# Awaiting the output's landing behind the closing barrier of the block instead of inside it

## The chip, the cores and the metric

The kernel runs on one core of one Trainium2 chip. The metric is the device time of one execution in microseconds (us), which is a little longer than the span of the profile: the span reaches from the first to the last of the program's own instructions, and the time also has what the runtime runs around them. Before the change the median of four runs is 420.90 us (420.85 to 422.17).

Five engines work side by side, each on its own stream of instructions: TensorE (PE in the profile, with its weight loads as PEld), VectorE (DVE), ScalarE (ACT), GpSimd (POOL) and SyncE (SP). They are ordered by semaphores alone. SP computes nothing here; it issues every transfer (DMA) of the kernel.

## What is computed

One decoding step of a transformer block for two sequences: a conditioned layer norm, attention of 32 query heads over a cache of 32768 positions in 4 groups, an output projection, a second conditioned layer norm and a two-layer mixer with gelu.

```python
mod = (_silu(c) @ w_mod).reshape(2, 6, 1, -1)      # sa, ca, ga, sb, cb, gb
h = _layernorm(x) * (1 + ca) + sa
x = x + ga * _A_ref(h, k_cache, v_cache, wq, wo)   # softmax(q k^T / sqrt(128)) v, then wo
h = _layernorm(x) * (1 + cb) + sb
return x + gb * _B_ref(h, w1, b1, w2, b2)          # gelu(norm(h) w1 + b1) w2 + b2
```

The caches are 2 x 4 x 32768 x 128 in bf16 for keys and values each, which with the weights makes 178.28 MB to be read. The output is 2 x 1 x 1024 in bf16, 4 KB.

## The kernel before

The program is recorded first and emitted afterwards. A `Tracker` takes each operation with the regions that it reads and writes, works out the semaphore waits, and keeps a list for each of the five engines. At the end `T.emit(block)` (line 734) writes every list into its engine's section of one block, opened at line 733. Each engine's section ends in a branch to a common closing part. There the engines meet in a barrier: PE, DVE, ACT and SP each count up a "gather" semaphore, POOL waits until it has all four, then counts up a "release" semaphore, on which the four leave. This closing part is written by the block itself, so the profile gives its instructions line 733. A barrier of the same build stands at the program's start, under line 748.

The work falls into a head (conditioning vector, first layer norm, projection to queries), a loop over the 8 pairs of sequence and group, in which PE, DVE and ACT each run the same recorded round, and a tail (output projection, second layer norm, mixer). SP's list is straight: it issues the loads in order, each as soon as the part of the buffer that it overwrites is free.

The tail is the part that the change touches. The last weights arrive on SP's queue as four tiles of `w2`; the last 12 of the 28 rows of blocks are multiplied at line 719 into `psO`. Then comes a chain in which each step waits for the one before: line 722 multiplies by the gate (DVE), line 723 adds the residual (DVE), line 724 transposes through PE, line 726 copies the 16 x 128 result to `res16`, which lies in the place of the input `c` and so is named `c` in the profile. SP waits for that copy and issues the one transfer to the output (line 730), whose landing counts the semaphore `s_out` up to 16. The next entry of SP's list, line 731, waits for `s_out` to reach 16. It is the last in SP's section, and in the built program this wait is carried by SP's branch out of the section, so the profile shows it under line 733. What follows it on SP is the closing barrier.

```python
T.wait("sp", reads=["res16"])
T.raw("sp", lambda e: e.dma_start(out..., res16[:, :]).then_inc(s_out, 16))   # line 730
T.raw("sp", lambda e: e.wait_ge(s_out, 16))                                   # line 731
with nc.Block() as block:                                                     # line 733
    T.emit(block)                                                             # line 734
```

Of the kernel before, what the change touches and what calls it, by code (L numbers as in the profile page):

```python
# [233 lines left out]
def bass_adaLN_cond__gqa_block_cached__mixer_channel_mlp__decode_kernel(  # L234
# [15 lines left out]
    T = Tracker(nc)  # L250
# [477 lines left out]
    s_out = nc.alloc_semaphore("s_out")  # L728
    T.wait("sp", reads=["res16"])
    T.raw("sp", lambda e: e.dma_start(out.rearrange("b o (k p) -> (b o k) p", p=128), res16[:, :]).then_inc(s_out, 16))  # L730
    T.raw("sp", lambda e: e.wait_ge(s_out, 16))

    with nc.Block() as block:
        T.emit(block)


# [26 lines left out]
```

## Time and profile before

| What | us | Where it is read |
|---|---|---|
| Median of four runs | 420.90 | the times |
| The profiled execution's own time | 420.84 | the times |
| Its span | 419.04 | the views of the trace by stretch |
| Time outside the span | 1.80 | the difference |
| PE busy | 282.1 | the page, part 1 |
| DVE busy | 169.5 | the page, part 1 |
| ACT busy | 167.6 | the page, part 1 |
| POOL busy | 6.8 | the page, part 1 |
| Stretch 40 to 375 us: DMA share 1.00, 433 GB/s | 335.0 | the stretches |
| Stretch 413.00 to 417.30 us: PE 3.11 busy, DMA share 0.38 | 4.30 | the stretches |
| Stretch 417.30 to 419.04 us: no compute engine busy, DMA share 0.01 | 1.74 | the stretches |

The profile is of one execution. "Busy" counts compute instructions alone; branches, waits on semaphores and the issue of transfers are work of an engine's sequencer and stand under the engine's name with a q behind it (SPq, POOLq). The last stretch of the table therefore shows nothing in the compute columns although something takes place in it: it is seen only in the view of one source line and in the view of waits.

### The profile page before, as it was taken

The page shows a single profiled execution, that of the slowest core. Times are in us where ns is not written, and L with a number is a line of the kernel's source. Part 1 is how long each engine was busy: PE and PEld are TensorE (multiplying, and loading weights), DVE is VectorE, ACT ScalarE, POOL GpSimd, SP SyncE. Part 2 cuts the span into 40 slices and gives each one's busy share as a digit, 9 for nine tenths or more (in the row PEclk, how much of TensorE's full clock was granted, in tenths as well). Part 3 has the DMA queues.
Part 4 walks back from the last instruction along what each step waited for, and adds up shares of the span by engine and source line. Part 5 has one row for each costly group of instructions (what it writes and reads, how often), then busy time and mean ns, then how long its engine had stood idle before and what let it go on. Part 6 is the DMA issues. An engine that isn't in the chain of part 4 may idle for free.

```text
span 419.0 us, 11662 instructions
## 1 busy us (share of the span) xinstructions
PE 282.1 (67%) x5183; PEld 223.7 (53%) x5183; DVE 169.5 (40%) x351; ACT 167.6 (40%) x275; POOL 6.8 (2%) x29
## 2 busy tenths in 40 slices
PE   1407439855992898389559928974894699274456
PEld 1104219842991498169529915972793299122324
DVE  1201105641772377157417724760673177220421
ACT  2000015544566165526545662645465266600100
POOL 3000000000000000000000000000000000000000
PEclk9976568966996799599869968995997699686565
DMA  9989999999999999999999999999999999999995
GB/s 376 450 378 446 447 404 488 409 400 445 460 413 429 438 435 429 438 435 457 410 416 475 432 394 447 460 413 429 454 419 429 438 435 457 404 422 441 416 435 232
DMA packets 5583, 178.43 MB, mean 426 GB/s; under 512 B 699, under 2 KB 707, under 8 KB 965
## 3 DMA queue, kind: packets, MB, share of 16 engines
q1 hardware_dynamic: 5572, 178.28, 98.7%
q8 instruction: 8, 0.13, 0.1%
q14 instruction: 3, 0.02, 0.0%
HBM read 178.28 MB, written 0.00 MB: 425 GB/s over the span
## 4 chain that ended last, share of the span: by engine, by line
PE 56%; DMA 22%; ACT 7%; issue 7%; DVE 7%; SPq 0%; ACTq 0%
PE psKT L534 29%; PE psZ L576 11%; DMA K<-in_A_k_cache_dram 10%; DMA w<-in_B_w_dram 9%; PE psS L546 6%; PE psZ L546 5%; ACT E_sb L566 4%; DMA wmod<-in_w_mod_dram 4%; DVE msum L591 2%; ACT KT_sb L538 2%; DVE m1c L551 1%; ACT S_sb L550 1%; PE psM L584 1%; PE psM L562 1%; PE psM L596 1%
## 5 line engine op out<-in xcount | busy, mean ns | idle before, releaser
L534 PE MATMUL psKT<-ident,K 128*128 128x128 bf16 x2048 | 154.7, 221 | 4.6 <-DMA K<-in_A_k_cache_dram 4.6
L538 ACT ACTIVATE KT_sb<-psKT 128x1024 bf16<-128x1024 bf16 x96 | 97.7, 1025 | 115.2 <-PE psKT L534 115.2
L540 DVE COPY KT_sb<-psKT 128x1024 bf16<-128x1024 bf16 x160 | 106.3, 688 | 44.1 <-PE psKT L534 43.1
L534 PEld LDWEIGHTS psKT<-ident,K 128*128 128x128 bf16 x2048 | 118.9, 98 | 5.8 <-DMA K<-in_A_k_cache_dram 4.7
L546 PE MATMUL psS<-qcur,KT_sb 128*128 128x8 bf16 x1024 | 44.3, 167 | 1.6 <-issue 1.6
L576 PE MATMUL psZ<-V,E_sb 128*32 128x512 bf16 x512 | 44.9, 528 | 0.0
L546 PE MATMUL psZ<-qcur,KT_sb 128*128 128x8 bf16 x1024 | 43.0, 167 | 0.7
L566 ACT ACTIVATE E_sb<-S_sb,negm 128x256 bf16<-128x256 f32 x64 | 32.5, 508 | 25.0 <-DVE negm L563 23.2
L546 PEld LDWEIGHTS psS<-qcur,KT_sb 128*128 128x128 bf16 x1024 | 39.2, 96 | 1.6 <-issue 1.6
L546 PEld LDWEIGHTS psZ<-qcur,KT_sb 128*128 128x128 bf16 x1024 | 37.9, 97 | 1.8 <-ACT KT_sb L538 1.2
L584 PE MATMUL psM<-onesf,rsum 128*128 128x1 f32 x16 | 4.7, 361 | 45.3 <-DVE rsum L583 45.3
L576 PEld LDWEIGHTS psZ<-V,E_sb 128*32 128x32 bf16 x512 | 17.0, 128 | 24.0 <-issue 20.0
L584 PEld LDWEIGHTS psM<-onesf,rsum 128*128 128x128 f32 x16 | 4.0, 309 | 46.1 <-DVE rsum L583 46.1
L589 DVE TENSOR_SCALAR msum<-psZ,mk 128x128 f32<-128x128 f32 x8 | 2.8, 351 | 43.1 <-PE psZ L576 43.1
L583 DVE COPY rsum<-rowsum 128x128 f32<-128x128 f32 x8 | 1.8, 227 | 41.4 <-ACT E_sb L566 41.4
L467 PE MATMUL psS<-wmod,inT 128*32 128x512 bf16 x32 | 4.9, 597 | 16.1 <-DMA wmod<-in_w_mod_dram 16.1
L551 DVE TENSOR_REDUCE m1c<-psZ 128x8 f32<-128x512 f32 x16 | 11.1, 693 | 10.3 <-ACT S_sb L550 10.3
L596 PE MATMUL psM<-msum,hmat 128*128 128x128 f32 x16 | 3.9, 326 | 13.0 <-DVE msum L591 13.0
L434 ACT ACTIVATE stat<-stat 128x2 f32<-128x2 f32 x3 | 0.6, 204 | 29.7 <-DVE stat L433 29.7
L551 DVE TENSOR_REDUCE m1c<-psS 128x8 f32<-128x512 f32 x16 | 11.1, 693 | 3.2 <-ACT S_sb L550 3.1
L557 PE MATMUL psM<-identf,m 128*8 128x128 f32 x16 | 3.4, 296 | 13.1 <-DVE m L554 13.1
L550 ACT ACTIVATE S_sb<-psZ 128x512 f32<-128x512 f32 x16 | 9.5, 595 | 6.3 <-PE psZ L546 6.3
(121 smaller groups left out, 173.0 us busy)
## 6 DMA issues: line engine op xcount, KB each, us to landing
K<-in_A_k_cache_dram SPq DMA_DIRECT2D x16, 4096.0 KB, 25.1
wq<-in_A_wq_dram SPq DMA_DIRECT2D x2, 4096.0 KB, 45.0
wo<-in_A_wo_dram SPq DMA_DIRECT2D x2, 4096.0 KB, 36.4
w<-in_B_w_dram SPq DMA_DIRECT2D x2, 3584.0 KB, 30.6
wmod<-in_w_mod_dram SPq DMA_DIRECT2D x1, 6144.0 KB, 29.7
w<-in_B_w_dram SPq DMA_DIRECT2D x3, 2048.0 KB, 35.5
wmod<-in_w_mod_dram SPq DMA_DIRECT2D x1, 4608.0 KB, 15.7
wmod<-in_w_mod_dram SPq DMA_DIRECT2D x1, 1536.0 KB, 5.9
```

The lines of the kernel that those rows point to most:

```text
L467: pe(lambda e, w=it.view, k=k, kk=kk, ch=ch, n=n, q=q: e.matmul(bank[n][32 * q:32 * q + 32, :], lhsT=inT[:, k, :], rhs=w[:, kk, ch * 512:( ...
L534: pe(lambda e, kq=kq, jj=jj, w=kt, t=t: e.transpose(psKT[kq][:, jj * 128:(jj + 1) * 128], w[:, t, :], ident[:, :]), reads=[it.reg, "ident" ...
L538: act(lambda e, src=src: e.activation(KT_sb[g8][:, :, :], src, ACT.Copy), reads=[f"psKT{kq}"], writes=[f"KT_sb{g8}"], sem=f"ev{cc}_{g8}")
L540: dve(lambda e, src=src: e.tensor_copy(KT_sb[g8][:, :, :], src), reads=[f"psKT{kq}"], writes=[f"KT_sb{g8}"], sem=f"ev{cc}_{g8}")
L546: pe(lambda e, t=t, jj=jj: e.matmul(ps[:, t * HPG:(t + 1) * HPG], lhsT=KT_sb[g8][:, jj, :], rhs=qcur[:, :], start=True, stop=True), reads= ...
L550: act(lambda e: e.activation(Sc, ps.rearrange("p (t h) -> p h t", h=HPG), ACT.Copy), reads=[preg], writes=[f"S_sb_{cc}"], sem=f"sc{cc}")
L551: dve(lambda e: e.tensor_reduce(m1c[:, :, cc], ps.rearrange("p (t h) -> p h t", h=HPG), AX.X, ALU.max), reads=[preg], writes=[f"m1c{cc}"])
L566: act(lambda e: e.activation(E_sb[:, :, h, :], S_sb[:, h, :].rearrange("p (u t) -> p u t", t=4), ACT.Exp, bias=negm[:, h:h + 1], scale=SCA ...
L576: pe(lambda e, t4=t4, tg=tg, q=q: e.matmul(psO[32 * q:32 * q + 32, :], lhsT=E_sb[:, tg // 4, :, :].rearrange("p h t -> p (h t)"), rhs=vt[: ...
L584: pe(lambda e: e.matmul(psM[:, 144:145], lhsT=rsum16.rearrange("p g h e -> p (g h e)"), rhs=onesf[:, 0:1], start=True, stop=True), reads=[ ...
L591: dve(lambda e, q=q: e.scalar_tensor_tensor(out=msum[:, :], in0=psO[:, q * 128:(q + 1) * 128], scalar=mk4[:, q:q + 1], in1=msum[:, :], op0 ...
L596: pe(lambda e: e.matmul(psM[:, 256:384], lhsT=hmat.rearrange("p g h e -> p (g h e)"), rhs=msum[:, :], start=True, stop=True), reads=["hmat ...
```

## The change

Line 731 is taken out of SP's list. The wait for `s_out` is now an instruction of its own on SP, behind the block and so behind the block's closing barrier. The block is opened with `no_gpsimd_drain=True`.

```diff
     T.raw("sp", lambda e: e.dma_start(out.rearrange("b o (k p) -> (b o k) p", p=128), res16[:, :]).then_inc(s_out, 16))
-    T.raw("sp", lambda e: e.wait_ge(s_out, 16))
-
-    with nc.Block() as block:
+
+    with nc.Block(no_gpsimd_drain=True) as block:
         T.emit(block)
+    nc.sync.wait_ge(s_out, 16)
```

In the built program the two differ in the closing part alone. Before, PE, DVE, ACT and SP each have one DRAIN there, which itself waits for the release semaphore to be zero and counts up the gather semaphore, and one semaphore instruction (EVENT_SEMAPHORE) that waits for the release; POOL has a DRAIN and two semaphore instructions. After, each of the four has a bare DRAIN, then a semaphore instruction that counts up the gather, then the one that waits for the release; POOL has its two semaphore instructions and no DRAIN; and SP has, as its last, the wait for `s_out`. SP's branch carries no wait any more. All that stands ahead of the closing part is the same on every engine, in the same order.

## Prediction

> **What bounds the kernel now.** I read the page first, for the bulk:
>
> ```profile
> DMA  9989999999999999999999999999999999999995
> q1 hardware_dynamic: 5572, 178.28, 98.7%
> ```
>
> The sixteen DMA engines are busy in every slice but the last, 98.7% of the span on SP's queue. The kernel is bound by reading 178.28 MB; no line of that part is touched. Only the last slice ends on something else, so I went on to the timeline of the end (start, duration, engine, line):
>
> ```profile
> 413.31 2.84 PE L719 MATMUL psZ<-gT,w 128*128 128x2 bf16 x96 [0.39 <-DMA w<-in_B_w_dram]
> ...
> 416.18 0.17 DVE L722 TENSOR_TENSOR mT<-psZ,modT 128x16 f32<-128x16 f32 x1 [5.19 <-PE psZ L719]
> ...
> 416.99 0.28 DVE L726 CAST c<-psM 16x128 bf16<-16x128 f32 x1 [0.37 <-PE psM L724]
> 417.29 0.35 SPq L730 DMA_DIRECT2D out_dram<-c  x1
> ```
>
> From 413.31 all is one chain: last matmuls, two DVE steps, a transpose, a copy, and the output's issue at 417.29. There the timeline stops, but the span runs to 419.04. The view of SP's own waits and that of line 730 show what fills the 1.75 us:
>
> ```profile
> SPq L733 <- DMA out_dram<-c: 1.0, 1, 1.0
> SPq L733 <- PEq L733: 0.2, 1, 0.2
> ```
> ```profile
> DMA to landing us min/median/max: 1.4/1.4/1.4
> ```
>
> The transfer lands 1.4 us after the start of its issue, at 418.7; the issue itself took 0.35, so SP stood 1.0 us at its branch. The view of line 733 (count, then shortest/median/longest in ns, then starts) has the closing part:
>
> ```profile
> L733 POOLq EVENT_SEMAPHORE  x2: 17/17/17, 418.9 to 418.9; - x2
> L733 POOLq DRAIN  x1: 341/341/341, 374.8 to 374.8; - x1
> L733 ACTq DRAIN  x1: 279/279/279, 404.0 to 404.0; - x1
> L733 PEldq DRAIN  x1: 325/325/325, 416.7 to 416.7; - x1
> L733 DVEq DRAIN  x1: 316/316/316, 417.0 to 417.0; - x1
> L733 SPq COMPARE_BRANCH  x1: 33/33/33, 418.7 to 418.7; - x1
> L733 SPq DRAIN  x1: 7/7/7, 418.8 to 418.8; - x1
> L733 SPq EVENT_SEMAPHORE  x1: 17/17/17, 419.0 to 419.0; - x1
> ```
>
> The order in time is the point. POOL, ACT, PE and DVE arrive at the barrier at 375.1, 404.3, 417.0 and 417.3 and wait. SP is last: branch at 418.7, DRAIN at 418.8, POOL's two instructions at 418.9, release at 419.0. The barrier lies wholly behind the landing, in series with it.
>
> **The change, part by part.**
>
> The wait leaves SP's branch. Branch, DRAIN and barrier then follow the issue at once. The issue ends at 417.29 + 0.35 = 417.64. From the branch to the end of the barrier the rows show 419.04 - 418.67 = 0.37 us (the trace's records give the branch's start as 418.670 and the end as 419.041). So the barrier is over near 417.64 + 0.37 = 418.01, and with the added semaphore instruction on SP near 418.05; I price that one at 0.04 us, between its own 17 ns and the 78 ns between the starts of POOL's two in the same records. DVE, the last of the others, has arrived at 417.3, and its own added instruction at some 0.04 keeps it well ahead of SP. The cover over all this is the landing, due at 418.65 (the sixteenth count of the output's semaphore); 0.6 us of it are left. If that cover were gone, the added instructions would cost some 0.1 us.
>
> The wait comes back behind the barrier. SP reaches it near 418.05, and the landing ends it at 418.65; a semaphore instruction takes 17 ns and starts as the branch did, 17 ns after the last count. New end of the span: 418.67 + 0.02 = 418.69. **Inside the span: 419.04 - 418.69 = 0.35 us less.** Queued behind the waiting instruction on SP is nothing of the program, only the runtime's closing code, and for SP's arrival in that the other engines wait. The output's transfer is issued at the same time, past no other transfer.
>
> The drain left out on POOL: 341 ns at 374.8, 44 us before the end, under the DMA-bound tail. Nothing, either way. The same goes for PE, DVE and ACT, where DRAIN and count are now two instructions.
>
> Outside of the span lie 420.84 - 419.04 = 1.80 us, which no row of the views shows. Bounds: if the runtime's closing takes as long from SP's end as before, the gain stays 0.35. But four engines now leave near 418.05, 0.64 us ahead of SP, and can do their share of arriving in the runtime's own closing barrier under the landing. Here a rule is weighed. The trace's semaphore records run on past the span: the runtime's barrier counts one semaphore nine times from 419.28 to 419.82, 0.54 us, and the same nine counts after the semaphores' reset take 0.36 (420.61 to 420.96). The Trainium skill's "Runtime: NRT & Kernel Launch", section "The ~15µs preamble/postamble breakdown", prices the closing barrier at about 1.5 us, the reset at 1.5 and the last barrier at 2, 5 us in all; by it, up to 1.5 us of "wait for all engines" might be had. The records leave 0.54 for that barrier, of which 0.18 is more than the second takes (one count comes after 0.21 instead of 0.04). I take the records: a late arrival of one engine costs at most 0.18 plus the hops ahead of SP, say 0 to 0.3, **0.15 taken**, since which engine is late isn't told by them. Sum: 0.35 + 0.15 = 0.50 us.
>
> The second rule speaks against the change. The skill's "Runtime: NRT & Kernel Launch", "Instruction fetch mechanics", says that a taken branch to a target outside the fetched window has to fetch it before going on. The row: 33 ns of branch, then DRAIN 0.16 us after the branch's start. By the rule a fetch would cost something like the 1.4 us of the output's small transfer (an estimate), and SP's barrier would end near 417.64 + 1.4 + 0.25 = 419.3, past the landing and 0.25 later than now: 421.2. Before, such a fetch could have hidden in the wait that the branch carried only if the fetch needs no decision of the branch. By the row it ends at 418.05. I take the row: the branch goes to the same place, and the 0.16 us after it stood behind the wait.
>
> **Forecast.** The profiled 420.84 would become 420.34. The median stands 0.06 above it, so I say 420.4.
>
> **Rivals.**
>
> *SP's DRAIN sees the output in flight.* The drains of PE, DVE and ACT last 279 to 325 ns because they wait for their engine's last instruction (DVE's from 417.00 to 417.32, the copy ending at 417.27). SP's took 7 ns, but with every transfer landed. If SP's drain holds until its transfer is done, the barrier is in series again: drain over at 418.7, POOL and release 0.21 as before, plus 0.1 for the added instructions: 419.0, no gain. If it waits for more than the semaphore's last count, the Trainium skill's "DMA: Bandwidth & Descriptors" with its fixed cost of about 2.0 us for a transfer against the 1.4 measured gives 417.29 + 2.0 + 0.31 = 419.60: 0.56 slower, **421.5 us**, below the 0.3% line. It decides against the change from a drain of about 0.9 us on (417.8 to 418.7). Against it: the same page says that landing is told by the completion semaphore, and no row shows SP's sequencer knowing of a transfer otherwise. Its milder form gives 420.9.
>
> *The runtime's closing is hidden much further.* If the four early engines could also reset their semaphores under the landing, only SP's own reset and the last barrier would follow 418.69. In the records the resets fill 419.71 to 420.38, and SP's share can't be above that; some 0.9 us more would go, **419.5**. Against it: the nine counts ahead of the resets are a barrier, which SP's late arrival must hold.
>
> *Nothing shows in the time.* The span is shorter by 0.35 but the time ends on something with its own clock: **420.9**. For it only that the 1.80 us are not itemized.
>
> *The tail grows in a way no row has*, such as a fetch behind the moved wait plus a repeated closing: more than 1.3 us, **422.2**. One of the four runs of before was 422.17, so scatter can give this too.
>
> **How the numbers follow.** About 0.3%, 1.26 us, is what a measurement of this kernel can tell from no change. Forecast (420.2 to 420.6): 0.68. Drain holds SP: 0.12. Hidden further: 0.06. Nothing: 0.07. Growth or scatter above: 0.07. The range takes the first, the milder half of the second, the fourth, and the fetch that the rule would price: 420.0 to 421.2, leaving out about 0.19. Faster by over 0.3% is the third case where it reaches 1.26, and scatter: 0.06. Slower by over 0.3%: 0.07. The rest, 0.87, lies within.
>
> **What would show it.** After, SP's branch and DRAIN near 417.6 to 417.8, POOL's two instructions near 417.9, the release near 418.0, and one SP semaphore instruction with a wait of some 0.6 us on the output's transfer, ending the span at 418.7 if the bulk takes as long. It is wrong if SP's DRAIN is longer than 0.1 us, if the gap from the output's issue to the span's end stays at 1.75 instead of 1.4, or if time minus span grows from 1.80. The bulk's own length can differ between executions, so the stretch from 417.29 on is to be compared, not the span alone.

## The result and the profile after

The changed kernel takes **420.14 us** (median of 33 runs, 419.94 to 423.21), the kernel before in the same comparison 420.93 (53 runs). The ratio is 0.9981, with a 95% interval from 0.9975 to 0.9988: 0.8 us less (0.5 to 1.1), a fifth of a per cent. It is clear of no change, on the side that was forecast. The forecast was 420.4, 0.5 us less; 420.14 lies just below the band that it favoured (420.2 to 420.6) and inside its whole range (420.0 to 421.2).

The span of the profiled execution hardly tells of it. These are the first line and the DMA row of the page, after (the row is the same as before, slice by slice):

```profile
span 419.0 us, 11665 instructions
...
DMA  9989999999999999999999999999999999999995
```

The span was 419.0 before as well. But this execution issued its output later: here are the last two rows of the timeline (start, duration, engine, line).

```profile
417.27 0.28 DVE L726 CAST c<-psM 16x128 bf16<-16x128 f32 x1 [0.37 <-PE psM L724]
417.57 0.35 SPq L730 DMA_DIRECT2D out_dram<-c  x1
```

Before, the issue was at 417.29; now it is at 417.57. Those 0.28 us come from the bulk, which the change leaves alone, so each execution has to be measured from its own issue on. From the issue to the span's end it was 419.04 - 417.29 = 1.75 us, and it is 418.96 - 417.57 = 1.39.

SP's own waits, after (line, what it waited for, us in total, times, longest):

```profile
SPq L734 <- DMA out_dram<-c: 0.6, 1, 0.6
SPq L732 <- PEq L732: 0.2, 1, 0.2
```

The wait for the output is 0.6 us instead of 1.0, and stands on line 734, behind the barrier of line 732 and no longer ahead of it. The view of line 732, the closing part, and the row of line 734 (count, shortest/median/longest in ns, first and last start):

```profile
L732 DVEq EVENT_SEMAPHORE  x2: 21/21/21, 417.6 to 418.3; - x2
L732 SPq EVENT_SEMAPHORE  x2: 17/17/17, 418.2 to 418.3; - x2
L732 POOLq EVENT_SEMAPHORE  x2: 17/17/17, 418.2 to 418.3; - x2
...
L732 DVEq DRAIN  x1: 318/318/318, 417.3 to 417.3; - x1
L732 SPq DRAIN  x1: 124/124/124, 418.0 to 418.0; - x1
```
```profile
L734 SPq EVENT_SEMAPHORE  x1: 17/17/17, 418.9 to 418.9; - x1
```

The four counts of the barrier and its release are over at 418.3 to 418.4, while the output is still on its way; it lands at 418.93, and SP's wait at 418.94 is the last instruction of the program. POOL's drain is gone from the view, and so is the row of SP's branch, which now carries no wait. SP's drain has grown from 7 to 124 ns.

That is 0.36 us. The rest is outside of the span: the profiled execution took 420.26, so 420.26 - 418.96 = 1.30 us lie around it, against 1.80 before. Together 0.36 + 0.50 = **0.86 us** between these two executions, beside 0.8 between the medians. The 0.50 is no accident of one execution: over all runs of the kernel after, time less span is 1.31 us in the mean (1.25 to 1.35), and over the 35 runs of the kernel before in each later comparison 1.80 to 1.81 (1.75 to 1.85). So the larger part of the gain is not in any instruction of the program.

What runs there can be seen in the trace's records of semaphore updates, which go on past the span. There the runtime's closing barrier counts one semaphore, which no instruction of the program names, nine times; the step from one count to the next is called a hop below. The times are in us from the start of the output's issue:

```
                     1st   2nd   3rd   4th   5th   9th
before              1.988 2.022 2.234 2.278 2.301 2.525
after               1.050 1.084 1.294 1.338 1.505 1.669
```

Before, the program ended at 1.75 and all nine came after it. After, four of them come before the landing (1.36), and only five are left when SP is done at 1.39. From the ninth count to the last count of the runtime's last barrier it takes 1.14 us in both. My theory after this: the count is passed from engine to engine and back, SP is the fifth and turning one, and so a landing that SP alone waits for covers the arrival of all the others. The rivals are that the drain left out on POOL brings a part, and that it only matters how many engines arrive early, not which one is late.

### The profile page after: what moved, and what is told of

The parts are those of the page before. It is cut to its first block, busy times and chain, and to the rows that moved or that the text cites. A ratio compares the mean times of both kernels' runs of the same rounds, so it can differ in the third digit from the quotient of the medians.

```text
span 419.0 us, 11665 instructions
## 1 busy us (share of the span) xinstructions
PE 279.2 (67%) x5183; PEld 221.7 (53%) x5183; DVE 169.6 (40%) x351; ACT 167.9 (40%) x275; POOL 6.8 (2%) x29
## 4 chain that ended last, share of the span: by engine, by line
PE 56%; DMA 22%; ACT 8%; issue 7%; DVE 6%; SPq 0%; ACTq 0%
PE psKT L534 29%; PE psZ L576 11%; DMA K<-in_A_k_cache_dram 10%; DMA w<-in_B_w_dram 8%; PE psS L546 6%; PE psZ L546 5%; ACT E_sb L566 4%; DMA wmod<-in_w_mod_dram 4%; DVE msum L591 2%; ACT KT_sb L538 2%; DVE m1c L551 1%; ACT S_sb L550 1%; PE psM L584 1%; PE psM L562 1%; PE psM L596 1%
## 5 line engine op out<-in xcount | busy, mean ns | idle before, releaser
L566 ACT ACTIVATION_READ_ACCUMULATOR E_sb<-S_sb,negm 128x1 f32 x64 | 12.0, 187 | 0.0
```

Source lines behind the costliest of these rows:

```text
L566: act(lambda e: e.activation(E_sb[:, :, h, :], S_sb[:, h, :].rearrange("p (u t) -> p u t", t=4), ACT.Exp, bias=negm[:, h:h + 1], scale=SCA ...
```

## The experiments

For each kernel the table has, beside the median, three figures of its profiled execution: from the issue of the output to the span's end, the time outside of the span, and their sum, the profiled time less the start of the issue. The sum is free of the scatter of the bulk. Each ratio is to the runs of the kernel before in the same comparison; their medians were 420.93 for the change, 420.98 for the four rows below it and 420.89 for the last four. The intervals are wide, since a few runs of most kernels are 1 to 3 us above the rest, and two of the gains (wait moved alone, wait on POOL) are not clear of no change by them. Most differences here are told by the medians and the sums together, and by the time outside over all runs of a kernel, whose mean is within 0.03 us of the table's figure in every row.

| Kernel | Median | Ratio to before (95%) | Issue to span's end | Outside | Sum |
|---|---|---|---|---|---|
| before | 420.93 | | 1.75 | 1.80 | 3.55 |
| after | 420.14 | 0.9981 (0.9975 to 0.9988) | 1.39 | 1.30 | 2.69 |
| wait moved alone | 420.09 | 0.9983 (0.9965 to 1.0002) | 1.39 | 1.32 | 2.71 |
| POOL's drain left out alone | 421.01 | 1.0003 (0.9987 to 1.0020) | 1.82 | 1.79 | 3.61 |
| wait on ACT | 420.26 | 0.9980 (0.9971 to 0.9989) | 1.39 | 1.48 | 2.87 |
| wait on POOL | 420.58 | 0.9990 (0.9979 to 1.0002) | 1.38 | 1.86 | 3.24 |
| wait on PE | 420.39 | 0.9986 (0.9975 to 0.9996) | 1.43 | 1.58 | 3.01 |
| 8 counts ahead of the wait | 420.13 | 0.9984 (0.9971 to 0.9997) | 1.39 | 1.29 | 2.68 |
| 8 counts, kernel before | 420.92 | 0.9996 (0.9983 to 1.0009) | 2.17 | 1.37 | 3.54 |
| 40 counts ahead of the wait | 422.42 | 1.0037 (1.0024 to 1.0050) | 3.68 | 1.33 | 5.01 |

**The two parts of the diff apart.** First the wait is moved alone:

```diff
-    with nc.Block(no_gpsimd_drain=True) as block:
+    with nc.Block() as block:
         T.emit(block)
     nc.sync.wait_ge(s_out, 16)
```

> The wait is moved behind the block as in the change, but the block keeps its drain on POOL, so each engine's DRAIN carries the count again. Theory (the landing covers the barrier and the runtime's arrival, both through the moved wait): the whole gain is here, 0.8 us under before, 420.1; from the output's issue to the span's end 1.35 to 1.40 us instead of 1.75. Rival (leaving out POOL's drain, or the split of drain and count, brings a part): 0.2 us or more of the gain is missing, 420.4 or above.

The median is 420.09 and the sum 2.71: the whole gain is there. Ten of the twelve runs lie at or below 420.28, under the lowest of the 35 runs of before (420.73). Then POOL's drain is left out alone, in the kernel before:

```diff
-    with nc.Block() as block:
+    with nc.Block(no_gpsimd_drain=True) as block:
```

> The wait stays inside the block as before, only the drain on POOL is left out of the block. Theory: no gain; from the landing on the closing part is longer by the one added semaphore instruction on SP, so the time is 420.9 to 421.0, and SP's drain is 7 ns again since nothing is in flight. Rival (the drain left out brings a part): 420.7 or below.

It took 421.01, none of its runs is below the lowest of before, and the sum is 0.07 us longer, by the semaphore instruction that SP has more. The drains of SP on line 732 of the first and on line 733 of the second:

```profile
L732 SPq DRAIN  x1: 123/123/123, 417.8 to 417.8; - x1
```
```profile
L733 SPq DRAIN  x1: 7/7/7, 418.8 to 418.8; - x1
```

Both instructions follow everything else on SP; the one that starts 0.06 us after the end of the output's issue takes 123 ns, the one that runs after the landing 7. What the longer one waits for is open; it is over 0.83 us ahead of the landing. The rival of the drain falls: leaving it out brings nothing. The semaphore instruction that comes with it costs, if anything, the 0.07 us.

**Who waits.** The wait is given to another engine; the rest is as after the change.

```diff
-    nc.sync.wait_ge(s_out, 16)
+    nc.scalar.wait_ge(s_out, 16)
```

> As the change, but ACT waits for the output's landing instead of SP. Theory with places (the runtime's closing barrier passes a count from engine to engine, and SP stands at the turning point, so that all four ahead of it are done while it waits): ACT's late arrival holds all hops behind its own place, so 0.1 to 0.5 us of the 0.8 are lost, 420.2 to 420.7; the span is as short as after the change. Rival (only the number of engines that arrive early counts, four in both): 420.1, as after the change.

In the next kernels it is `nc.gpsimd.wait_ge` and `nc.tensor.wait_ge`.

> As the change, but POOL waits for the output's landing instead of SP. Theory with places: the trace of before and of after shows a gap of 0.21 us ahead of the third count of the runtime's closing barrier, in both, so one engine takes that much longer to arrive after the program's end; if it is POOL, its late arrival loses some 0.4 to 0.5 us of the 0.8, 420.5 to 420.7; if it isn't, the loss is that of its place, 0.1 to 0.4. Rival (place has no part): 420.1.

> As the change, but PE waits for the output's landing. The runs with the wait on ACT and on POOL delayed the second and the third count of the runtime's closing barrier, so the order is PE, ACT, POOL, DVE, SP. Theory with places: the first count is now late, all eight hops follow it. Taking the arrival of 0.29 us that PE has after the program's barrier and 0.54 us for the nine counts as before: last count at 1.39 + 0.23 + 0.54 or, with POOL already arrived, 0.36, so 0.3 to 0.5 us of the gain lost, 420.4 to 420.6. Rival (only POOL is dear): 420.1 to 420.2.

The span can't tell these apart: from the issue to its end they take 1.38 to 1.43 us, as after the change. The rows of line 734 with the wait on POOL and with the wait on PE:

```profile
L734 POOLq EVENT_SEMAPHORE  x1: 17/17/17, 418.7 to 418.7; - x1
```
```profile
L734 PEldq EVENT_SEMAPHORE  x1: 51/51/51, 418.8 to 418.8; - x1
```

The difference is all in the time outside: 1.30 us with the wait on SP, 1.48 on ACT, 1.58 on PE, 1.86 on POOL. Over all runs of each kernel these times do not overlap between SP (1.25 to 1.35) and any of the three (from 1.44 on). The semaphore records tell why. Again in us from the issue; the landing is at 1.34 to 1.36 in each:

```
                     1st   2nd   3rd   4th   5th   9th
wait on PE          1.629 1.663 1.701 1.746 1.769 1.996
wait on ACT         1.049 1.517 1.556 1.600 1.623 1.850
wait on POOL        1.049 1.083 1.922 1.965 1.989 2.214
wait on SP (after)  1.050 1.084 1.294 1.338 1.505 1.669
```

The count that is held shows the place of the engine that waits: PE is first, ACT second, POOL third, SP fifth, and DVE, which was not tried, is left for the fourth. Which engines make the last four counts no run shows; that it is the way back is taken from their number. From the start of its wait's instruction to its count an engine takes 0.13 us on SP, 0.14 on ACT, 0.25 on PE, and **0.55 on POOL**. So the place is one part of the loss (all hops behind the waiting engine come after the landing) and the engine's own way out is the other. ACT, which gets out as fast as SP, shows the place alone: its ninth count is 0.18 us later, and so is its sum. What fills POOL's 0.55 no record shows. With the wait on POOL, what is left of the gain is 420.98 - 420.58 = 0.40 us by the medians of that comparison, 0.31 by the sums: about the closing barrier of the block, and no more. That counting early engines alone decides is refuted: with four early in each case the times lie between 420.1 and 420.6. The losses on ACT (0.12 us by the medians, 0.18 by the sums) and PE (0.25 and 0.32) lie near the lower end of what was expected, that on PE below it by the medians.

**The cover.** Eight counts of a semaphore that nobody reads are put on SP between the barrier and the wait, and, for their price, at the end of the kernel before.

```diff
     s_out = nc.alloc_semaphore("s_out")
+    s_idle = nc.alloc_semaphore("s_idle")
...
         T.emit(block)
+    for _ in range(8):
+        nc.sync.sem_inc(s_idle, 1)
     nc.sync.wait_ge(s_out, 16)
```

> As the change, with eight semaphore counts on SP (of a semaphore that nobody waits for) between the closing barrier and the wait for the output. Price of one: 17 to 80 ns by the rows of single counts, so 0.14 to 0.64 us on SP. Theory (the landing is the last thing on SP and covers what stands ahead of it, with 0.59 us of cover left after the barrier): from the output's issue to the span's end still 1.39 us, time as after the change, 420.1. Rival (SP's own instructions set the end): longer by the price, 420.25 to 420.75.

> As before, with the same eight counts on SP behind the closing barrier, so behind the landing too. Both theories: nothing covers them there, and the price of eight counts shows in full: 1.75 us plus 0.14 to 0.64 from the issue to the span's end, and as much on the time, 421.1 to 421.6. It gives the price against which the run with the covered counts is read.

Ahead of the wait they cost nothing (420.13; sum 2.68), as the theory had it: the landing covers them, for they take up time that SP would have waited. These are their row and that of the wait behind them:

```profile
L736 SPq EVENT_SEMAPHORE  x8: 17/17/17, 418.1 to 418.5; - x8
```
```profile
L737 SPq EVENT_SEMAPHORE  x1: 17/17/17, 418.7 to 418.7; - x1
```

The second expectation fell. The rows of the counts, in the kernel before:

```profile
L737 SPq EVENT_SEMAPHORE  x8: 17/17/17, 419.2 to 419.6; - x8
```

Eight counts from 419.2 to 419.6, 58 ns apart in the records, all behind the landing and behind the barrier, and the span is longer by 0.42 us, 2.17 from the issue. Yet the time is 420.92, and the sum 3.54 as before. SP had 0.42 us to spare *after the end of the program*. It is the runtime's barrier again: its third count, POOL's, comes at 2.225 there, as at 2.234 before, and SP's turn is after it, at 2.302 as at 2.301. So the time before was not set by the last instruction of the span, but by POOL's 0.55 us from the release of the barrier on.

Forty counts ahead of the wait (the same edit with `range(40)`):

> As the change, with forty counts on SP between the barrier and the wait. Theory: the cover of 0.59 us is used up and the rest is exposed: 40 times the price found with eight counts, less 0.59 us, so 0.1 to 2.6 us above the change by the price of 17 to 80 ns, and the last wait finds the output landed. Rival (the runtime's own arrival has slack beyond the landing): less than that by more than 0.2 us.

The time is 422.42, 2.28 above the change; the sum is 2.32 above. By 58 ns for each, less the 0.59 us that the landing covers, it should be 1.7. The rest, 0.5 us, is in the counts themselves: in the records they run 58 ns apart, but the four gaps after the 26th are 104, 85, 463 and 81 ns. What held SP there is open: the one transfer of instructions that the records show in this stretch, of 8 KB, starts only at 3.57, after it. It isn't one odd execution either, for the lowest of the twelve runs is 422.30. The first four counts of the runtime stand at 1.05 to 1.34 as after the change, and the fifth, SP's, at 3.81: past what the landing covers, everything on SP is exposed, and no further slack follows.

No version was found that beats the changed kernel by more than the scatter (the wait moved alone is 0.05 us lower by the median and 0.02 higher by the sum). With the wait on SP the landing of 1.36 us is followed by 0.15 us to SP's count and four hops. POOL is not far behind even so: its count lets the fourth come at 1.34, so SP's could come at 1.36 instead of 1.505, and a landing earlier by more than some 0.14 us would bring nothing further (an estimate from these counts and the 0.023 us hop before SP's turn). Letting the output leave PSUM without the copy of line 726 (0.28 us) was not tried.

## Why the prediction was right, and where its size was off

*The bulk is untouched.* Right: the DMA row is the same as before.

*The barrier moves under the landing, 0.35 us.* Right: 1.75 became 1.39, 0.36 less, and the run with the wait moved alone has all of it. The barrier's end was put near 418.05 for an issue at 417.29, so 0.76 after it; it came 0.81 after it (418.386 less 417.572). Three terms make the 0.05: SP's drain took 0.12 more than the 7 ns of the working, the way from the issue to it 0.10 less, and the added semaphore instruction 0.07 instead of 0.04. The wait of 0.6 us that was left is what was forecast.

*The added instructions and POOL's drain cost nothing.* Right, the first because of the cover: with the wait ahead of the barrier the same instruction shows as 0.07 us.

*Outside the span, 0.15 us taken of 0 to 0.3.* The way was right, four engines arriving under the landing, but this is the term that was mis-sized: it measured **0.50**, 1.80 to 1.30, beyond the end that was kept. Said was that "a late arrival of one engine costs at most 0.18 plus the hops ahead of SP". The gap ahead of the third count was taken as the late engine's whole price. It is only what shows of it between two counts. Before, POOL's way out of 0.55 us began at the release and carried the chain to SP's fifth count, 0.62 us after the release. After, that whole stretch lies under the landing, and what follows SP's wait is SP's own 0.13. That is 0.49 us less; the last four hops are 0.16 instead of 0.22, which makes 0.55. Of it 0.05 lies inside the spans already, since the first span ends 0.06 after the release and the second 0.02 after the start of SP's wait: 0.50. Sum of the forecast with this term: 0.36 + 0.50 = 0.86. With the upper end of the term as it was kept, 0.3, the working comes to 420.25 at the lowest; that 420.14 still lay in the range is owed to its margin below the favoured band, which no term of the working fills.

*The rule on the closing barrier* (the Trainium skill's "Runtime: NRT & Kernel Launch", "The ~15µs preamble/postamble breakdown", 1.5 us for it) was rightly left for the records as a figure, but its description of it as a wait for all the engines was the better guide: it asks who is last, and the answer was POOL before and SP after.

*The rule on the taken branch.* No fetch showed: SP's drain starts 0.06 us after the end of the issue, and the last transfer of instructions in the trace starts 9.5 us before the issue.

*The rival with SP's drain.* It came true in small: right behind the output's issue the drain is 0.12 us longer, but it doesn't wait for the landing, and the cover swallows it. The 421.5 us needed a drain of 0.9. The 2.0 us that this rival took from the Trainium skill's "DMA: Bandwidth & Descriptors" is that page's fit for transfers issued from GpSimd ("Anatomy of one DMA — SWDGE (gpsimd) path"); here SP issues, and the output landed 1.36 us after the start of its issue.

*Hidden much further (419.5).* Not so, though not for the reason given: the resets don't wait for the ninth count. The first of them comes 0.12 us after the fifth count, SP's, both before (at 2.419, ahead of the ninth at 2.525) and after (at 1.625), and in each of the other traces as well. SP's turn still comes after the landing, and the 1.14 us from the ninth count to the last barrier's end are the same. *Nothing shows:* wrong, and the outside time, which this rival trusted to stay, fell the most. *The tail grows (422.2):* not so; four of the 33 runs after are above 421.0, up to 423.21, but the kernel before scatters as far, to 423.56.

*The signs that would show it wrong.* "If SP's DRAIN is longer than 0.1 us" came true, at 124 ns, while the prediction held: the sign was badly chosen, since SP had 0.6 us of cover for it. "If the gap from the output's issue to the span's end stays at 1.75" was the right one to watch; the span alone, 419.0 in both, would have misled.

## What to carry to other kernels

A kernel's last transfer is a wait that other closing work can lie under: let the engines meet first, and let one engine alone await the landing. Choose that engine by how fast it gets out and by who waits for it afterwards: SP was best here, POOL gave over half of the gain back. The end of the span isn't the end of the time: an instruction added at the end of the span was free, and one removed may be as well, so compare the time and the span of each run before such an edit is summed.

## What the runs showed of the hardware

- The runtime's closing barrier counts in the order PE, ACT, POOL, DVE (by elimination), SP, and then four times more. Unhindered, as in the last barrier, it takes 0.36 us for its eight hops; POOL needs 0.55 us from its last instruction to its count, SP 0.13.
- A DRAIN on SP took 7 ns when its transfers had landed and 123 to 124 ns right after the issue of one, in the seven runs with such a drain; it ended 0.83 us ahead of the landing.
- Semaphore counts of 17 ns each on SP follow each other 58 ns apart, so 17 ns isn't what one costs.
